# Products of p and v with the roles of the operands exchanged, in a kernel of attention and two expert layers

## Chip, cores, metric

The kernel runs on one core of a Trainium2 chip (trn2). The metric is the device time of one execution in microseconds; the median of several executions counts.

## What is computed

Attention keeps the 32 largest scores of each row, and its output goes through two layers. `B, heads, S, D` are 2, 8, 576, 64, so there are 1152 tokens of 512 features.

```python
scores = (q @ k.T) / sqrt(D)
kth = the 32nd largest score of each row
attn = softmax(where(scores >= kth, scores, -1e9))      # sum + 1e-9
x = attn @ v                       # (B, heads, S, D) -> (B * S, 512)

g = domain_probs / (sum(domain_probs) + 1e-9)
x = sum over e of g[:, e] * (relu(x @ w1[e]) @ w2[e])   # 4 experts, 1024 wide
out = max(x @ m1, x @ m2, x @ m3) @ mo                   # 768 wide
```

## The kernel before

**Pairs.** The tokens lie in nine tiles of 128, and tile 4 belongs half to each batch (it is the "mixed" tile). One unit of attention is a pair of heads for one tile: 36 pairs, class `Pair`, numbered 0 to 35 in the order of `pairs` (lines 371 and 372). The mixed tile's four pairs are numbers 16, 18, 20 and 21.

**Steps of a pair.** `scores` (TensorE, copied out by ScalarE); `topk`, seven VectorE steps for each head (max of 8 and replacement in turn, lines 444 and 446); `negate`, `exp` and `mask` make p and the sums of its rows; `trans_p` (lines 484 to 498) turns p in nine blocks of 128 x 128, and ScalarE copies them into `pt[0]`, `pt[1]` (four blocks each) and `pt[2]` (the last 64 keys of both heads together). `guard`, `recip` give the reciprocals `rr` of the sums, one for each token and head, tokens on partitions.

**Products with values, `pv`, lines 522 to 537.** The result stands transposed: partitions are the 2 x 64 features of the two heads, columns are tokens. v is the operand that stands in the array, p moves. The tail comes first, one matmul with 128 x 128 weights (`v_last`, block-diagonal), then for each of four blocks and two heads a matmul with 128 x 64 weights, whose results go to the partitions of that head:

```python
nc.tensor.matmul(ps[:, cols], lhsT=last, rhs=self.pt[2][:, cols], start=True, stop=False)
for r in range(NR):
    for j in range(2):
        nc.tensor.matmul(ps[j * D:(j + 1) * D, cols], lhsT=vs[:, j * NR + r, :],
                         rhs=self.pt[j][:, r, cols], start=False, stop=r == NR - 1)
```

A mixed pair does this twice, with 64 tokens of each batch. Since the result has features on partitions, the reciprocals have to be turned too: `spread` (line 513, ScalarE) repeats them to 128 x 128, `trans_r` (line 518, TensorE) transposes that, ScalarE copies it to `r` (line 520), and `norm` (line 542, VectorE) multiplies. `split_x` (lines 555 and 556) splits the result into a high part (ScalarE) and a low part (GpSimd), which lie in a ring of four tiles for the experts.

**Order.** Everything is issued in an order that the program fixes itself; each engine works through its queue in this order. `attention` counts in slots, eight for each pair, and puts every step at a slot from the pair's first: for most pairs (`LOOSE`, line 45) `recip` at 15, `pv` and `trans_r` at 17, the copy of r at 19, `norm` at 20, `split_x` at 21, with its GpSimd part at 23. `two` puts the second half of a step `lag` slots later. `last` says at which slot x of a pair counts as ready. The pairs 3, 7 and 11, the last of their tiles, and a few around them have tighter orders.

**Experts beside attention.** The first expert layer is a generator (`products`), from which the main loop (lines 992 to 1013) takes work slot by slot: the VectorE time that a slot books (`dve`) is added to a goal, and expert work is issued until the TensorE time it books (`pe`) reaches that goal. Where a stage needs x that isn't ready, nothing is issued and the goal's time is dropped. Stage c (1 to 6) works on tiles c − 1 and c, stages 7 and 8 on the last ones. Each product is three matmuls on split operands (`product`, lines 681 to 683). The second layer, with weights that VectorE, ScalarE and GpSimd convert after attention (`to_float32`), comes at the end. PSUM has six banks in one ring (tag "g") for all of these, and two for output sums.

Of the kernel before, what the change touches and what calls it, by code (L numbers as in the profile page):

```python
# [10 lines left out]
F32 = mybir.dt.float32  # L11
# [3 lines left out]
AF = mybir.ActivationFunctionType  # L15
ALU = mybir.AluOpType
# [11 lines left out]
WAITING = 2  # L28
# [6 lines left out]
ON_ACT = (range(2, 36), (2, 5, 6, 8, 9, 10, 12, 13, 14))  # L35
# [3 lines left out]
FIRST = dict(stag=2, new=1, scores=-12, trans=11, pv=17, rec=16, lag=2, sum=4, late=1)  # L39
MIDDLE = dict(stag=2, new=1, scores=-12, at=(11, 12), pv=14, rec=12, lag=1, sum=0, late=1)  # L40
TIGHT = dict(stag=3, new=1, scores=-7, at=(10, 11), guard=11, rec=11, spread=12, pv=12, turn=12, norm=13, split=13, last=14, lag=0, lag_s=1, sum=0, late=1)
SECOND = dict(TIGHT, norm=14, split=14, last=15)
THIRD = dict(stag=4, new=1, scores=-4, at=(11, 12), guard=12, rec=13, spread=13, pv=14, turn=14, norm=15, split=15, last=16, lag=0, lag_s=2, sum=0)
BOTH = dict(stag=4, new=1, scores=-4, at=(14, 14), pv=17, rec=15, lag=2, lag_t=1, sum=0, late=1)
LOOSE = dict(stag=4, new=1, scores=-4, at=(14, 14), pv=17, rec=15, lag=2, sum=0)

EARLY = 7

ALONE_FROM, ALONE_STEP = -8, 4
LOAD, LOAD_FULL = 11, 9  # L50
# [10 lines left out]
def kernel(  # L61
# [14 lines left out]
    nc = tc.nc  # L76
    B, HP, D, _, S = k.shape
    NT, DM = out.shape
    E = gates.shape[2]
    P = 128  # L80
# [3 lines left out]
    NR = S // P  # L84
# [27 lines left out]
    at = ctx.enter_context(tc.tile_pool(name="at", bufs=2))  # L112
# [7 lines left out]
    ident = const.tile([P, P], F32, name="ident")  # L120
# [9 lines left out]
    def dve(n):  # L130
        clock["dve"] += 0.07 + n / 960.0

    def pe(n):
        clock["pe"] += n / 2400.0

    def bank(name):
        return pg.tile([P, 512], F32, tag="g", name=name)
# [170 lines left out]
    kraw, kT, vt, qraw, qT = {}, {}, {}, {}, {}  # L308
# [85 lines left out]
    def split_waiting():  # L394
        while waiting and room(waiting[0].t):
            waiting.pop(0).split_x()()

    class Pair:
        def __init__(self, n):
            self.n = n  # L400
            self.c, self.hp, self.t = pairs[n]
            self.s, self.w, self.m, self.nb = {}, {}, {}, {}
            self.p = self.rs = None
            self.pt = {}

            self.did = set()

            self.on_pool = [n in ON_POOL[j] for j in range(2)]
            self.on_act = [n in ON_ACT[j] for j in range(2)]

        def scores(self, j):
            srcs = [(b, i) for i, b in enumerate(batches(self.t))]
# [109 lines left out]
        def pv(self):  # L522
            assert {("pt", i) for i in range(3)} <= self.did
            ps = bank("psv")
            pe((NR + 1) * 512)
            if self.t == MIXED:
                parts = [(0, slice(0, TAIL)), (1, slice(TAIL, P))]
            else:
                parts = [(0 if self.t < MIXED else 1, slice(0, P))]
            for b, cols in parts:  # L530
                vs, last = vt[b, self.hp]
                nc.tensor.matmul(ps[:, cols], lhsT=last, rhs=self.pt[2][:, cols], start=True, stop=False)
                for r in range(NR):
                    for j in range(2):
                        nc.tensor.matmul(ps[j * D:(j + 1) * D, cols], lhsT=vs[:, j * NR + r, :],
                                         rhs=self.pt[j][:, r, cols], start=False, stop=r == NR - 1)
            self.x = ps

        def norm(self):
            assert "r" in self.did  # L540
# [17 lines left out]
    def attention():  # L558

        NP = len(pairs)  # L560
        prs = {}
        later, between = {}, {}

        def options(n):
            return TIGHT if n == HP - 1 else SECOND if n == 2 * HP - 1 else MIDDLE if n in (HP - 2, 2 * HP - 3, 2 * HP - 2) else FIRST if n < 2 * HP else THIRD if n == 3 * HP - 1 else BOTH if n in ON_ACT[1] else LOOSE

        def at_slot(s, f, *a):
            later.setdefault(s, []).append((f, a))


        first_use = {}
        for n, (c, hp, t) in enumerate(pairs):
            for b in batches(t):
                if ("v", b, hp) not in first_use:
                    first_use["v", b, hp] = n
                    at_slot(8 * n + (options(n)["pv"] - 7 if b and hp else 0), load_v, b, hp)
                if t >= FULL:
                    first_use.setdefault(("k", b, hp), n)
            if t >= FULL:
                first_use.setdefault(("q", c, hp), n)  # L580
            elif n:
                o = options(max(0, n - 2))
                at_slot(max(8 * n + options(n)["scores"] - LOAD_FULL, 8 * (n - 2) + o["scores"] + o["stag"] + 1), load_full, n)
        free = {"k": -99, "q": -99}
        for key, n in first_use.items():
            if key[0] == "v":
                continue
            s0 = 8 * n
            load, split = (load_k, split_k) if key[0] == "k" else (load_q, split_q)
            at = max(s0 + options(n)["scores"] - (SPLIT_K if key[0] == "k" else SPLIT_Q), free[key[0]] + 2)  # L590
            if key[0] == "k" and key[1] and key[2]:

                at = max(at, 8 * pairs.index((MIXED, key[2] - 1, MIXED)) + options(n)["scores"] + options(n)["stag"] + (1 if key[2] == HP - 1 else 4))
            at_slot(max(at - LOAD, free[key[0]] + 1), load, *key[1:])
            at_slot(at, split, *key[1:])
            free[key[0]] = at
        for n, (c, hp, t) in enumerate(pairs):
            s0 = 8 * n
            prs[n] = Pair(n)
            pr = prs[n]  # L600
            o = options(n)

            def two(s, f, *a, lag=o["lag"]):
                at_slot(s, lambda: at_slot(s + lag, f(*a)))
            for j in range(2):
                b0 = s0 + o["stag"] * j
                two(b0 + o["scores"], pr.scores, j, lag=o.get("lag_s", o["lag"]))
                for i in range(7):
                    if o["new"]:
                        later.setdefault(b0 + i, []).insert(0, (pr.topk, (j, i)))  # L610
                    else:
                        at_slot(b0 + i, pr.topk, j, i)
                at_slot(b0 + 2, pr.negate, j)
                at_slot(b0 + 5, pr.exp, j)
                late = o.get("late", MASK_LATE) * pr.on_act[j]
                two(b0 + 7 + late, pr.mask, j, lag=o["sum"] if n < EARLY else 3)
                two(s0 + o["at"][j] if "at" in o else b0 + o["trans"] + late + (late > 0), pr.trans_p, j, lag=o.get("lag_t", o["lag"]))
            two(s0 + o["at"][1] if "at" in o else s0 + o["stag"] + o["trans"], pr.trans_p, 2, lag=o.get("lag_t", o["lag"]))
            at_slot(s0 + o.get("guard", o["rec"] - 1), pr.guard)
            at_slot(s0 + o["rec"], pr.recip)  # L620
            at_slot(s0 + o.get("spread", o["rec"] + 1), pr.spread)
            at_slot(s0 + o["pv"], pr.pv)
            two(s0 + o.get("turn", o["rec"] + 2), pr.trans_r)
            end = max(o["pv"], o["rec"] + 2) + o["lag"]
            if "norm" in o:
                between.setdefault(s0 + o["norm"], []).append((pr.norm, ()))
            else:
                at_slot(s0 + end + 1, pr.norm)
            two(s0 + o.get("split", end + 2), pr.split_x)
        last = {}  # L630
        for n, p in enumerate(pairs):
            o = options(n)
            last[p[0:2]] = 8 * n + o.get("last", max(o["pv"], o["rec"] + 2) + 2 * o["lag"] + 2)
        for n in range(len(alone)):
            at_slot(ALONE_FROM + ALONE_STEP * n, load_alone, n + 1)
        end = max(last.values()) + 1
        s = min(later)
        while s <= end:
            todo = later.pop(s, [])
            i = 0  # L640
            while i < len(todo):
                f, a = todo[i]
                f(*a)
                todo[i + 1:i + 1] = between.pop(s, [])
                todo += later.pop(s, [])
                i += 1
            yield s, [c for c in last if last[c] + (READY if c[1] == HP - 2 else 0) == s]
            s += 1

        while narrowed[0] < WIDE * len(wide):  # L650
            clock["dve"] += PAUSE
            yield s, []
            s += 1


    lag = []
# [424 lines left out]
```

## Time and profile before

| | |
|---|---|
| runs of the kernel, us | 751.1, 751.87, 753.61 |
| median, us | 751.87 |
| the profiled execution, us | 752.02 |
| its span, first to last instruction, us | 750.2 |
| granted clock of TensorE, mean | 0.997 |

The profile is of one execution. The span is shorter than that execution's own time by what lies around the instructions. A record is one instruction; busy time counts overlapping records of an engine once. PE is TensorE's matmul, PEld its weight load, DVE is VectorE, ACT ScalarE, POOL GpSimd. Starts of TensorE's records are the better guide: their ends are modelled. A number after L is the line of the kernel.

### The profile page before, as it was taken

How to read it: one execution, taken by the hardware profiler on the slowest of the kernel's cores; microseconds unless marked ns; L12 is line 12 of the kernel's file. 1: busy time of each engine (PE TensorE's matmuls, PEld its weight loads, DVE VectorE, ACT ScalarE, POOL GpSimd, SP SyncE). 2: the span in 40 equal slices, each digit the busy share in tenths (PEclk: the TensorE clock that was granted, in tenths of full speed). 3: DMA queues.
4: the chain of work that ended last, by engine and by line, in shares of the span. 5: the costliest groups of instructions: out<-in, count | busy, mean ns of one | idle time of the engine just before them, and what ended most of it. 6: DMA issues, size and time to landing. Idle time of an engine off the chain costs nothing. (4 is left out here: it accounts for less than half of the span.)

```text
span 750.2 us, 13770 instructions
## 1 busy us (share of the span) xinstructions
PE 721.8 (96%) x4758; PEld 642.7 (86%) x4758; DVE 579.1 (77%) x1161; ACT 508.0 (68%) x1137; POOL 495.2 (66%) x432
## 2 busy tenths in 40 slices
PE   6799999999999999999999998999999899999998
PEld 3576788888989989898989977899989799999996
DVE  6999989989999899999999964887778544233341
ACT  4668889899978787788788856576656633433531
POOL 2514778679979797697778659888768743442520
PEclk9999999999999999999999999999999999999999
DMA  7584565535647364445444355889979742453501
GB/s 221 179 267 158 154 183 159 154 127 159 192 123 212 110 189 124 149 134 166 134 132 153 114 183 168 298 297 301 297 239 314 257 149 82 151 172 99 195 4 42
DMA packets 56487, 130.16 MB, mean 173 GB/s; under 512 B 9761, under 2 KB 23329, under 8 KB 56417
## 3 DMA queue, kind: packets, MB, share of 16 engines
q1 hardware_dynamic: 48064, 120.69, 51.5%
q10 hardware_dynamic: 8352, 8.59, 3.2%
q8 instruction: 37, 0.61, 0.3%
q14 instruction: 34, 0.27, 0.1%
HBM read 120.60 MB, written 8.65 MB: 172 GB/s over the span
## 5 line engine op out<-in xcount | busy, mean ns | idle before, releaser
L278 POOL TENSOR_TENSOR wlo<-raw,whi 128x512 fp32r<-128x512 f32 x258 | 340.4, 1348 | 119.4 <-ACT whi L272 115.9
L272 ACT ACTIVATE whi<-raw 128x1024 fp32r<-128x1024 f32 x164 | 169.7, 1056 | 36.2 <-PE ps L683 12.9
L681 PE MATMUL ps<-xl,whi 128*128 128x256 f32 (+1 forms) x584 | 173.7, 297 | 0.4 <-POOL xl L556 0.4
L683 PE MATMUL ps<-xh,wlo 128*128 128x256 f32 (+1 forms) x584 | 170.8, 292 | 0.0
L682 PE MATMUL ps<-xh,whi 128*128 128x256 f32 (+1 forms) x584 | 170.7, 292 | 0.0
L444 DVE MAX8 m<-work 128x8 f32<-128x576 f32 x216 | 155.2, 745 | 0.1
L681 PEld LDWEIGHTS ps<-xl,whi 128*128 128x128 f32 x584 | 110.8, 190 | 1.7 <-POOL xl L556 0.6
L682 PEld LDWEIGHTS ps<-xh,whi 128*128 128x128 f32 x584 | 109.7, 188 | 0.8 <-issue 0.2
L683 PEld LDWEIGHTS ps<-xh,wlo 128*128 128x128 f32 x584 | 109.8, 188 | 0.0
L278 DVE TENSOR_TENSOR wlo<-raw,whi 128x1024 fp32r<-128x1024 f32 x35 | 56.2, 1606 | 66.3 <-ACT whi L272 48.9
L446 DVE MATCH_REPLACE8 work<-m,work 128x576 f32<-128x576 f32 x144 | 106.7, 742 | 0.0
L681 PE MATMUL ps<-wlo,h 128*128 128x512 f32 x224 | 91.1, 406 | 0.9 <-POOL wlo L278 0.9
L683 PE MATMUL ps<-whi,h 128*128 128x512 f32 x224 | 87.9, 393 | 3.5 <-POOL h L818 3.5
L682 PE MATMUL ps<-whi,h 128*128 128x512 f32 x224 | 87.8, 392 | 0.0
L431 ACT ACTIVATE s<-pss 128x288 f32<-128x288 f32 x144 | 51.2, 399 | 11.6 <-PE pss L419 11.1
L444 DVE MAX8 m<-s 128x8 f32<-128x576 f32 x72 | 53.8, 748 | 5.0 <-ACT s L431 5.0
L249 POOL TENSOR_TENSOR narrow<-narrow,raw 128x256 int32<-128x256 int32 x48 | 44.2, 927 | 17.1 <-DVE narrow L246 4.4
L683 PEld LDWEIGHTS ps<-whi,h 128*128 128x128 f32 x224 | 42.1, 188 | 13.9 <-POOL h L818 4.4
L446 DVE MATCH_REPLACE8 work<-m,s 128x576 f32<-128x576 f32 x72 | 53.4, 742 | 0.0
L681 PE MATMUL ps<-x2l,whi 128*128 128x384 f32 x144 | 49.1, 341 | 2.1 <-DVE x2l L908 2.1
L681 PEld LDWEIGHTS ps<-wlo,h 128*128 128x128 f32 x224 | 42.9, 192 | 9.1 <-POOL wlo L278 2.7
L683 PE MATMUL ps<-x2h,wlo 128*128 128x384 f32 x144 | 49.0, 341 | 0.0
(113 smaller groups left out, 1472.3 us busy)
## 6 DMA issues: line engine op xcount, KB each, us to landing
raw<-in_w_dram SPq DMA_DIRECT2D x128, 512.0 KB, 4.2
raw<-narrow SPq DMA_DIRECT2D x36, 512.0 KB, 4.0
raw<-in_m_dram SPq DMA_DIRECT2D x36, 256.0 KB, 4.7
whole<-in_w_dram SPq DMA_DIRECT2D x14, 512.0 KB, 5.4
narrow<-narrow ACTq DMA_DIRECT2D x48, 128.0 KB, 4.8
kraw<-in_k_dram SPq DMA_DIRECT2D x16, 288.0 KB, 4.5
qraw<-in_q_dram SPq DMA_DIRECT2D x48, 64.0 KB, 3.9
raw<-in_mo_dram SPq DMA_DIRECT2D x12, 256.0 KB, 4.7
```

The costliest lines, as they stand in the source:

```text
L249: nc.gpsimd.tensor_tensor(out=out.bitcast(I32), in0=out.bitcast(I32), in1=last, op=ALU.add)
L272: nc.scalar.activation(out=hi, in_=raw, func=AF.Copy)
L278: on.tensor_tensor(out=lo[:, x], in0=raw[:, x], in1=hi[:, x].bitcast(F32), op=ALU.subtract)
L431: nc.scalar.activation(out=s[:, h, :], in_=halves[h][:, 0:SH], func=AF.Copy)
L444: nc.vector.max(m[:, 8 * r:8 * r + 8], src)
L446: nc.vector.match_replace(out=self.w[j], in_to_replace=m[:, 8 * r:8 * r + 8], in_values=src, imm_value=NEG)
L681: nc.tensor.matmul(ps, lhsT=lh, rhs=rl, start=first, stop=False)
L682: nc.tensor.matmul(ps, lhsT=lh, rhs=rh, start=False, stop=False)
L683: nc.tensor.matmul(ps, lhsT=ll, rhs=rh, start=False, stop=last)
```

## The change

For the 26 pairs from number 8 on, but for 10 and 11, p's turned blocks stand in the array and v moves, 64 columns for a head. The result has tokens on partitions, so that `rr` scales it directly (`norm_tokens`); it is then transposed (`trans_x`) and copied by ScalarE. Such pairs have no `spread` and no `trans_r`. Their steps come at `pv` + 2 (multiplication), + 4 (transposition, copied `lag` slots later) and + 7 (split); x counts as ready at `pv` + 9. `options` is moved out of `attention` unchanged.

```diff
+TOKENS_FROM = 8
+TOKENS = dict(norm=2, turn=4, split=7, last=9)
...
+            self.tokens = n >= TOKENS_FROM and n not in (3 * HP - 2, 3 * HP - 1)
...
+            self.x = ps
+            if self.tokens:
+                for b, cols in parts:
+                    nc.tensor.matmul(ps[cols, 0:P], lhsT=self.pt[2][:, cols], rhs=vt[b, self.hp][1], start=True, stop=False)
+                for r in range(NR):
+                    for j in range(2):
+                        for b, cols in parts:
+                            nc.tensor.matmul(ps[cols, j * D:(j + 1) * D], lhsT=self.pt[j][:, r, cols],
+                                             rhs=vt[b, self.hp][0][:, j * NR + r, :], start=False, stop=r == NR - 1 and j == 1)
+                return
...
-            self.x = ps
+
+        def norm_tokens(self):
+            self.xn = at.tile([P, 2, D], F32, tag="rb", bufs=1, name="xn")
+            dve(P)
+            nc.vector.tensor_tensor(out=self.xn, in0=self.x[:, 0:P].rearrange("p (j d) -> p j d", j=2), in1=self.rr.unsqueeze(2).to_broadcast([P, 2, D]), op=ALU.mult)
+
+        def trans_x(self):
+            ps = bank("psr")
+            pe(260)
+            nc.tensor.transpose(ps[:, 0:P], self.xn.rearrange("p j d -> p (j d)"), ident)
+
+            def copy():
+                self.xt = at.tile([P, P], F32, tag="xt", bufs=2 + WAITING, name="xt")
+                nc.scalar.activation(out=self.xt, in_=ps[:, 0:P], func=AF.Copy)
+                self.did.add("x")
+            return copy
...
+            at_slot(s0 + o["pv"], pr.pv)
+            if pr.tokens:
+                at_slot(s0 + o["pv"] + TOKENS["norm"], pr.norm_tokens)
+                two(s0 + o["pv"] + TOKENS["turn"], pr.trans_x)
+                two(s0 + o["pv"] + TOKENS["split"], pr.split_x)
+                continue
             at_slot(s0 + o.get("spread", o["rec"] + 1), pr.spread)
-            at_slot(s0 + o["pv"], pr.pv)
             two(s0 + o.get("turn", o["rec"] + 2), pr.trans_r)
...
-            last[p[0:2]] = 8 * n + o.get("last", max(o["pv"], o["rec"] + 2) + 2 * o["lag"] + 2)
+            last[p[0:2]] = 8 * n + (o["pv"] + TOKENS["last"] if prs[n].tokens else o.get("last", max(o["pv"], o["rec"] + 2) + 2 * o["lag"] + 2))
```

## Rows read from the trace of the kernel before

**Rows 1.** The page, part 1: busy us, share of the span, instructions of each engine.

```profile
PE 721.8 (96%) x4758; PEld 642.7 (86%) x4758; DVE 579.1 (77%) x1161; ACT 508.0 (68%) x1137; POOL 495.2 (66%) x432
```

**Rows 2.** Busy time by stretch: length, PE, PEld, DVE, ACT, POOL, clock, DMA.

```profile
100.00:450.00 350.00, 342.41 (x2620) 307.89 (x2619) 326.46 (x695) 289.54 (x693) 277.97 (x246) 1.00 0.52 155
450.00:750.20 300.20, 292.08 (x1615) 270.48 (x1613) 161.18 (x265) 149.77 (x258) 174.98 (x140) 0.99 0.58 191
```

**Rows 3.** Waits, 100 to 447 us: who <- for whom: us, times, longest.

```profile
ACT rb L513 <- DVE rr L509: 25.8, 15, 3.1
ACT xh L555 <- DVE xt L542: 22.7, 17, 2.3
...
PE psv L532 <- ACT pt L498: 3.1, 4, 1.5
...
PE psp L495 <- ACT raw L816: 1.5, 2, 0.8
```

**Rows 4.** Timeline, TensorE, an ordinary pair's products: start, length, record, count.

```profile
251.42 0.38 PE L532 MATMUL psv<-pt,v_last 128*128 128x128 f32 x2
...
251.73 1.09 PE L535 MATMUL psv<-pt,vt 128*64 128x128 f32 x16
...
252.75 0.33 PE L518 MATMUL psr<-ident,rb 128*128 128x128 f32 x1
...
252.84 0.36 PE L681 MATMUL ps<-xl,whi 128*128 128x256 f32 x1
...
253.04 0.28 PE L682 MATMUL ps<-xh,whi 128*128 128x256 f32 x1
```

**Rows 5.** Timeline, TensorE, a mixed pair's products.

```profile
240.73 0.33 PE L532 MATMUL psv<-pt,v_last 128*128 128x64 f32 x2
240.99 0.69 PE L535 MATMUL psv<-pt,vt 128*64 128x64 f32 x16
241.61 0.43 PE L532 MATMUL psv<-pt,v_last 128*128 128x64 f32 x2
...
242.67 0.48 PE L681 MATMUL ps<-wlo,h 128*128 128x512 f32 x1
```

**Rows 6.** Weight loads: two in that pair (timeline), and their group.

```profile
241.61 0.30 PEld L532 LDWEIGHTS psv<-pt,v_last 128*128 128x128 f32 x2
...
L532 PEld LDWEIGHTS psv<-pt,v_last 128*128 128x128 f32 x80 | 12.8, 192 | 9.6 <-ACT pt L498 7.8 <-issue 0.5 <-ACT s L431 0.2
```

**Rows 7.** Timeline, TensorE, transpositions of p and the matmuls after them.

```profile
247.97 1.03 PE L490 MATMUL psp<-ident,p 128*128 128x128 f32 x8
248.84 0.27 PE L495 MATMUL psp<-ident,p 128*128 128x128 f32 x1
248.87 0.49 PE L681 MATMUL ps<-wlo,h 128*128 128x512 f32 x1
249.19 0.39 PE L682 MATMUL ps<-whi,h 128*128 128x512 f32 x1
```

**Rows 8.** TensorE's groups by form: busy us, mean ns of one; idle before.

```profile
L766 PE MATMUL psa<-xfull,whole 128*128 128x128 f32 x128 | 16.1, 279 | 0.8 <-ACT pt L493 0.8
...
L535 PE MATMUL psv<-pt,vt 128*64 128x64 f32 x128 | 5.5, 228 | 0.0
...
L532 PE MATMUL psv<-pt,v_last 128*128 128x64 f32 x16 | 3.2, 279 | 0.2 <-ACT pt L498 0.2
```

**Rows 9.** Groups by form: the spread on ScalarE, the multiplication on VectorE.

```profile
L513 ACT ACTIVATE rb<-rr 128x128 f32<-128x128 f32 x36 | 11.3, 313 | 29.5 <-DVE rr L509 29.2
...
L542 DVE TENSOR_TENSOR xt<-psv,r 128x128 f32<-128x128 f32 x32 | 8.7, 273 | 4.3 <-ACT r L520 4.3
```

**Rows 10.** TensorE's groups from 100 to 450 us: one transposition for each pair.

```profile
L518 PE MATMUL psr<-ident,rb 128*128 128x128 f32 x28 | 9.2, 328 | 0.0
```

**Rows 11.** Timeline: the low part of tile 4's last x; stage 4's first matmul.

```profile
283.65 0.46 POOL L556 TENSOR_TENSOR xl<-xt,xh 128x128 fp32r<-128x128 f32 x1 [2.56 <-ACT xh L555]
...
285.30 0.36 PE L681 MATMUL ps<-xl,whi 128*128 128x256 f32 x1
```

More of the change, by code (lines that the diff above doesn't have):

```diff
@@ L396, in split_waiting, with options @@
             waiting.pop(0).split_x()()
+    def options(n):
+        return TIGHT if n == HP - 1 else SECOND if n == 2 * HP - 1 else MIDDLE if n in (HP - 2, 2 * HP - 3, 2 * HP - 2) else FIRST if n < 2 * HP else THIRD if n == 3 * HP - 1 else BOTH if n in ON_ACT[1] else LOOSE
     class Pair:
@@ L562, in attention @@
         later, between = {}, {}
-        def options(n):
-            return TIGHT if n == HP - 1 else SECOND if n == 2 * HP - 1 else MIDDLE if n in (HP - 2, 2 * HP - 3, 2 * HP - 2) else FIRST if n < 2 * HP else THIRD if n == 3 * HP - 1 else BOTH if n in ON_ACT[1] else LOOSE
         def at_slot(s, f, *a):
```

## Prediction

> **What bounds the kernel now.** The page's busy shares come first: TensorE is busy for 721.8 of the span's 750.2 us, the next engine for 579.1 [rows 1]. A high share alone proves little, so the second view is busy time by stretch. From 100 to 450 us, where the attention of 28 pairs runs beside expert products, TensorE is busy for 342.4 of 350 us; from 450 us, when attention is over, for 292.1 of 300.2 [rows 2]. So there are only 7.6 us of idle time on TensorE in the stretch that the change touches, and work that is added to TensorE has nowhere to hide: the expert products that it pushes back come out at the end of the program. The third view, the waits of the same stretch, says how much of that idle time ScalarE causes: TensorE waits 3.1 us for copies of the transposed p and 1.5 us for a bank that ScalarE empties late. ScalarE itself stands 25.8 us before the spread of the reciprocals and 22.7 us before the split of x, both times for VectorE [rows 3].
>
> One execution carries all durations: its own time is 752.0 us, 1.8 us over its span, and 0.15 us over the median of the three runs, 751.87; I forecast against 752.0.
>
> **The products with values, ordinary pair** (22 of the 26 pairs). Each float32 matmul shows as two records, each with a weight load of its own. Now: the pair at 251.42 us issues one matmul with the tail of v (2 records, 128 columns of the array) and eight with v (16 records, 64 columns of the array each, the two heads side by side), then the transposition of the spread reciprocals; the next expert matmul starts at 252.84 and is 0.08 us longer than its neighbour (0.36 against 0.28), since it waits inside [rows 4]. The whole is 252.84 − 251.42 + 0.08 = **1.50 us**. The 16 records take 252.75 − 251.73 = 1.02 us, some 0.06 each, because two stream side by side.
>
> After: p stands still, so all 18 records load 128 x 128 float32 weights, and 64 columns stream past. Halving the columns helps only if loading is not the limit. The trace of before has this very shape: in a mixed pair the tail matmul loads 128 x 128 float32 weights for 64 columns. From its start to the first value matmul 240.99 − 240.73 = 0.26 us pass [rows 5]; with 128 columns it is 251.73 − 251.42 = 0.31 [rows 4]. Two records with 64 columns fewer each, at the 0.11 that a 128-column record takes (248.84 − 247.97 over 8) [rows 7], should have saved 0.11; they saved 0.05, one record's worth. The second record waited for its load. The loads say the same: two of 0.19 us take 0.30 together, so one ends 0.11 after the other [rows 6], and nothing streamed long enough there to hold the second back. And these 64-column records last 279 ns on average, where 64-column records with half the weights last 228 [rows 8].
>
> So I take 0.11 us a record: 18 x 0.11 = 1.98 us. Then the transposition of x, now by itself. The nearest row is the last one of p: 248.87 − 248.84 = 0.03, and the matmul behind it is 0.09 longer (0.49 against 0.40), so 0.12 [rows 7]. Together **2.10 us, 0.60 more than now; 22 pairs: +13.2 us**. Bounds for a record: 0.055, if streaming alone counted (half of 0.11; it gives a rival below), and 0.126, the mean of the 128-column records of L766, 16.1 us over 128 [rows 8], which adds 22 x 18 x 0.016 = 6.3 us. I stay at 0.11, the row with the same weights.
>
> The Trainium skill (TensorE: Matmul & The Clock Gate, Back-to-back issue gap) gives the isolated spacing of matmuls by the streamed columns alone, so that half the columns are half the time; its section LDWEIGHTS gives a load by its columns over 1.2 GHz, 107 ns for 128. By the first the sum would come to about 741 us, by the second (18 x 0.107 + 0.12 a pair) to about 761.5, both estimates from the page. The rows of loads agree with the second.
>
> **Mixed pairs** (4). Now 242.67 − 240.73 + 0.08 = 2.02 us [rows 5, 7]. After, the two batches take the two halves of the array, with the same 64-column weights as now, and the two entries into this arrangement become one. Entry 0.09 (the 0.31 of the tail matmul before v's records, less two of 0.11) [rows 4]; four tail records two by two, 0.22; 32 records with one leaving, 2 x 0.62 − 0.14 = 1.10 (0.62 from 240.99 to 241.61; leaving is 1.02 less 8 x 0.11 in the ordinary pair) [rows 4, 5]; transposition 0.12. Together 1.53: **4 x −0.49 = −2.0 us.** If the new order of the 32 records loses the side-by-side streaming they take 32 x 0.055 = 1.76 instead of 0.96, and the four pairs cost +1.2 in all; I take −2.0, since neighbours still go to different halves.
>
> **What leaves and enters elsewhere.** The spread (0.31 us of ScalarE) goes in 26 pairs, and with it the wait for the reciprocal ahead of it; the copy of r becomes a copy of x, the same shape; the split then reads what ScalarE itself wrote, so its wait for VectorE goes too [rows 3, 9]. That is 26 x 0.31 = 8.1 us of work and most of 48.5 us of standing still, on an engine that isn't the bound. It counts only where TensorE waits for ScalarE: 3.1 + 1.5 us [rows 3]. Bounds 0 and −4.6; I take **−2.0**. The multiplication on VectorE keeps its shape (0.27 us, one factor now repeated along the row) [rows 9], moves one slot earlier and waits for the products instead of the copy of r; what queues behind it are the top-k steps of the next pairs, which TensorE must not come to need. It now also books 0.203 us in the planner's VectorE clock, 5.3 us in 26 pairs, which pulls as much expert work forward into attention; that moves work and adds none. No DMA is added or moved within a pair.
>
> **x later.** Transposition and split move x of a token pair from slot 23 to slot 26 after its pair's start. There are 28 pairs in 350 us [rows 10], so 12.5 us for a pair's 8 slots, and three slots are 4.7 us. Who waits is the next expert stage. Where x has time, this costs nothing; stage 4, however, begins at 285.30, 1.2 us after the last low part of tile 4 is written (283.65 + 0.46) [rows 11]. In the 3.5 us beyond this margin TensorE has only the attention's own work, roughly a third of its time by the pattern of scores, transpositions and products; so 0 to 2.3 us of idling. I take **+1.0**, because a TensorE that runs later than the plan spends part of it catching up. After the last pair, nothing stands between products and transposition, so TensorE waits for the multiplication of 0.27 us and its hand-over: **+0.5**, between 0 and 1.
>
> Sum: 752.0 + 13.2 − 2.0 − 2.0 + 1.0 + 0.5 = 762.7, so **763 us**.
>
> **Rivals.**
> - *Loads hide, streaming counts* (the other side). For it: the starts of the two 64-column records can't be told apart from a streaming cadence in a row that merges them, and loads do overlap matmuls everywhere. Against it: the 0.26, 0.30 and 279 above. A pair would take 18 x 0.055 + 0.12 = 1.11 us; 22 x −0.39 = −8.6, and with the other terms 752.0 − 8.6 − 2.0 − 2.0 + 1.5 = 741 us. The sign turns at 0.083 us a record: there 22 x (18 x 0.083 + 0.12 − 1.50) = 2.5 us, what the other terms (−2.5) give back. This is what the skill's rule on the issue gap would give (TensorE: Matmul & The Clock Gate). Chance 0.09.
> - *The idle time takes it.* TensorE fills all of its 7.6 idle us [rows 2] with the added work and the late x costs nothing: 752.0 + 13.2 − 2.0 − 7.6 = 755.6, and with records of 0.105, 753.6, no change that can be told. For it: ScalarE's freed 48 us. Against it: only 4.6 of the waits are ScalarE's. Chance 0.05, 0.04 of it within 0.3%.
> - *The late x decides.* Stage 4 pays its full 2.3, the multiplication on VectorE waits for slower products and holds up the top-k behind it once in most pairs, and records cost 0.115: 762.7 + 1.3 + 22 x 18 x 0.005 + 1 = 767 us. For it: the 1.2 us at stage 4 [rows 11]. Against it: the multiplication still comes two slots, 3.1 us, after the products, which grow by half a microsecond. Chance 0.12.
> - The forecast itself: 0.74. That the change does something else than it says is not a case: the loads, their shapes and the 26 pairs are plain from the code.
>
> **The numbers.** The likeliest case gives 763. The range runs from 755, where idle time takes most of it, to 769, where the late x or the higher price of a record decides; the faster rival is left out. About 0.3% (2.3 us) is what a measurement of this kernel can tell from no change. Faster 0.09, same 0.04, slower 0.87.
>
> **What would show it.** Right: the records of the new products stand 0.11 us apart and their loads touch each other without gaps; a token pair takes about 2.0 us on TensorE before it turns to other work; TensorE's busy time rises by about 11 us, while idle time in attention shrinks a little; spread and its 25.8 us of waiting are gone but for a few pairs; attention ends 15 us or so later, the rest is shorter. Wrong: records 0.06 apart (the first rival), a stop of TensorE by 285 to 300 us for x of 2 us or more (the third), a mixed pair above 2.0 us (side-by-side streaming lost).

## The result and the profile after

The changed kernel takes 763.37 us (median; 761.29 to 765.17), the kernel before 752.74 us beside it: a ratio of 1.0139, 95% interval 1.0106 to 1.0172. It is slower by 10.6 us, and the forecast of 763 us holds. The profiled execution took 765.17 us, with a span of 763.4 us, so its rows show some 2 us more than the median.

First come the products of an ordinary pair, in the timeline of TensorE and its weight loads (start, length, record, count). L541 is the tail's matmul and L545 the eight with v.

```profile
256.79 0.32 PEld L541 LDWEIGHTS psv<-v_last,pt 128*128 128x128 f32 x2
256.92 0.39 PE L541 MATMUL psv<-v_last,pt 128*128 128x128 f32 x2
257.03 1.87 PEld L545 LDWEIGHTS psv<-vt,pt 128*128 128x128 f32 x16
...
257.14 1.90 PE L545 MATMUL psv<-vt,pt 128*128 128x64 f32 x16
...
258.82 0.19 PEld L717 LDWEIGHTS ps<-xl,whi 128*128 128x128 f32 x1
258.85 0.36 PE L717 MATMUL ps<-xl,whi 128*128 128x256 f32 x1
```

From 256.92 to 258.85 us, 18 records take 1.93 us, 0.107 each. The row of loads has 16 loads of 0.19 us in 1.87 us with no break: (1.87 − 0.19) / 15 = 0.112 from one to the next. Loads are now back to back, and streaming seems to wait for them (the first experiment tests it). Before, the same work took 1.33 us up to the transposition [rows 4]. A mixed pair, whose weights have 64 columns, is quicker than before: 273.63 − 272.33 = 1.30 us, with the transposition still to come, against 1.94 us that hold the transposition [rows 5]:

```profile
272.33 0.44 PE L541 MATMUL psv<-v_last,pt 128*64 128x128 f32 x4
272.60 1.10 PE L545 MATMUL psv<-vt,pt 128*64 128x64 f32 x32
273.63 0.39 PE L717 MATMUL ps<-xl,whi 128*128 128x256 f32 x1
```

Then the page and busy time by stretch (columns as in [rows 1, 2]).

```profile
PE 737.6 (97%) x4758; PEld 665.2 (87%) x4758; DVE 580.4 (76%) x1161; ACT 509.2 (67%) x1111; POOL 494.3 (65%) x432
```

```profile
100.00:450.00 350.00, 344.58 (x2540) 318.65 (x2539) 323.33 (x683) 283.59 (x653) 277.84 (x244) 1.00 0.50 150
...
100.00:465.00 365.00, 357.70 (x2634) 330.43 (x2633) 329.96 (x700) 291.75 (x674) 280.42 (x248) 1.00 0.50 148
465.00:763.40 298.40, 291.73 (x1615) 270.19 (x1613) 160.59 (x264) 150.09 (x257) 172.78 (x140) 0.99 0.59 193
```

TensorE's busy time rose by 15.8 us, where the forecast had about 11, and VectorE's hardly at all. (The version with 128 columns below, whose profile has a mean clock of 0.997 like the one of before, is busy for 733.9 us, 12.1 more; the profile here, at 0.995, holds more slow records.) In the same 350 us TensorE idles for 5.4 us instead of 7.6, but attention now lasts until some 465 us, and up to there it idles for 7.3: idle time took up next to nothing. Behind attention the same 1615 matmul records stand in 298.4 us, and in 300.2 before [rows 2]: attention has grown by some 15 us, and the end moved with it.

ScalarE's two long waits, 25.8 and 22.7 us [rows 3], are gone but for 1.0 and 1.6 us in the groups from 100 to 450 us. New is a wait of 10.2 us for the transposition of x:

```profile
L588 ACT ACTIVATE xh<-xt 128x128 fp32r<-128x128 f32 x27 | 8.5, 314 | 2.1 <-DVE xt L575 1.6
L568 ACT ACTIVATE xt<-psr 128x128 f32<-128x128 f32 x24 | 6.7, 279 | 10.2 <-PE psr L564 10.2
L521 ACT ACTIVATE rb<-rr 128x128 f32<-128x128 f32 x2 | 0.6, 314 | 1.0 <-DVE rr L517 1.0
```

TensorE's own waits from 100 to 465 us show what that is worth to it. Those for copies of p are down to 1.8 us from 3.1, and that for a bank that ScalarE empties to 0.4 from 1.5 [rows 3]:

```profile
PE ps L717 <- POOL xl L589: 2.4, 2, 1.7
PE psv L541 <- ACT pt L506: 1.6, 2, 1.1
...
PE psp L503 <- ACT raw L852: 0.4, 1, 0.4
PE psv L550 <- ACT pt L506: 0.2, 1, 0.2
```

Stage 4, which began 1.2 us after its x [rows 11], now waits for it. The timeline of TensorE, with idle time and its releaser in brackets:

```profile
292.95 0.28 PE L718 MATMUL ps<-xh,whi 128*128 128x256 f32 x1
293.06 0.28 PE L719 MATMUL ps<-xh,wlo 128*128 128x256 f32 x1
295.05 0.56 PE L717 MATMUL ps<-xl,whi 128*128 128x256 f32 x1 [1.72 <-POOL xl L589]
295.42 0.42 PE L718 MATMUL ps<-xh,whi 128*128 128x256 f32 x1
295.63 0.41 PE L719 MATMUL ps<-xh,wlo 128*128 128x256 f32 x1
```

After the wait the same matmuls stand 0.21 us apart instead of 0.11. The row of the stretch shows why: the granted clock (third from the end) is 0.58 on average from 296 to 299 us, so TensorE ran mostly at the lower of its two levels, 1.2 GHz.

```profile
296.00:299.00 3.00, 3.00 (x18) 3.00 (x17) 2.78 (x6) 2.78 (x5) 3.00 (x3) 0.58 0.02 5
299.00:302.00 3.00, 3.00 (x27) 3.00 (x27) 2.73 (x6) 2.06 (x6) 3.00 (x3) 1.00 0.58 175
```

### The profile page after: what moved, and what is told of

Read it like the earlier page. It is cut to its first block, busy times and chain, and to the rows that moved or that the text cites. A ratio compares the mean times of both kernels' runs of the same rounds, so it can differ in the third digit from the quotient of the medians.

```text
span 763.4 us, 13738 instructions
## 1 busy us (share of the span) xinstructions
PE 737.6 (97%) x4758; PEld 665.2 (87%) x4758; DVE 580.4 (76%) x1161; ACT 509.2 (67%) x1111; POOL 494.3 (65%) x432
## 4 chain that ended last, share of the span: by engine, by line
PE 89%; ACT 4%; issue 3%; POOL 3%; DVE 1%; DMA 0%; ACTq 0%; POOLq 0%
PE ps L717 21%; PE ps L719 20%; PE ps L718 20%; PE psv L545 5%; PE pss L432 4%; PE psp L498 4%; PE pss L427 3%; PE psa L802 2%; PE pso L717 2%; PE pso L718 2%; PE pso L719 2%; PE psv L553 1%; PE ps L817 1%; POOL wlo L281 1%; PE psv L541 1%
## 5 line engine op out<-in xcount | busy, mean ns | idle before, releaser
L501 ACT ACTIVATE pt<-psp 128x512 f32<-128x512 f32 x72 | 39.8, 595 | 16.9 <-PE psp L498 16.8
```

Of the source, the lines that this page charges most:

```text
L501: return lambda: [nc.scalar.activation(out=d, in_=ps.rearrange("p (r n) -> p r n", r=NR), func=AF.Copy), self.did.add(("pt", part))]
```

## The experiments

**Is it the load or the streaming?** Two kernels change only how many columns pass each block of p in the 22 ordinary pairs: 32 (the other half of each head's v is left out) or 128 (the v of both heads) instead of 64.

```diff
-                            nc.tensor.matmul(ps[cols, j * D:(j + 1) * D], lhsT=self.pt[j][:, r, cols],
-                                             rhs=vt[b, self.hp][0][:, j * NR + r, :], ...)
+                            n = D // 2 if len(parts) == 1 else D
+                            nc.tensor.matmul(ps[cols, j * D:j * D + n], lhsT=self.pt[j][:, r, cols],
+                                             rhs=vt[b, self.hp][0][:, j * NR + r, 0:n], ...)
```

> The changed kernel, but in the 22 ordinary pairs only 32 of the 64 columns of each head stream past the standing blocks of p (the other 32 get the tail's part alone, so part of the products is left out). Theory (a record waits for its 128 x 128 weight load, 0.107 us whatever streams): the 18 records still take 1.92 us, the time stays at 763 us within 2. Rival (the 0.107 us are the streaming of 64 columns): 16 records of 0.053 us, 0.85 us less a pair, 22 pairs: 745 us.

```diff
+                            if len(parts) == 1:
+                                nc.tensor.matmul(ps[cols, 0:P].rearrange("p (j d) -> p j d", j=2), lhsT=self.pt[j][:, r, cols],
+                                                 rhs=vt[b, self.hp][0][:, r::NR, :], ...)
+                                continue
```

> The changed kernel, but in the 22 ordinary pairs 128 columns (both heads of v) stream past each block of p instead of 64, so each head's result also gets the products of the other head's p. Theory (load-bound): streaming 128 columns takes 0.109 us a record, as long as the load, so the 18 records take 1.92 to 1.96 us and the time stays at 763 to 764 us. Rival (streaming sets 0.107 us for 64 columns): 0.213 us a record, 16 x 0.107 x 22 = 38 us more, 801 us.

With 32 columns the median is 765.13 us (ratio 1.0168, 1.0141 to 1.0195), with 128 columns 761.76 us (1.0128, 1.0111 to 1.0145). The small difference goes against the number of columns, and three of the four runs with 32 columns had a low mean granted clock (0.989 to 0.991): at 0.995 the two took 762.51 and 761.98 us. The timelines of both, 32 columns first:

```profile
319.87 1.87 PE L546 MATMUL psv<-vt,pt 128*128 128x32 f32 x16
321.57 0.47 PE L718 MATMUL ps<-wlo,h 128*128 128x512 f32 x1
```

```profile
317.72 1.95 PE L546 MATMUL psv<-vt,pt 128*128 128x128 f32 x16
319.42 0.48 PE L721 MATMUL ps<-wlo,h 128*128 128x512 f32 x1
```

Sixteen records take 1.70 us with 32 columns, 1.70 with 128, and 1.71 with 64 in the changed kernel. So 32 to 128 columns cost the same, and the forecast's reading of the two tail records [rows 5] was right: streaming doesn't set the pace; by it the two kernels would have lain 56 us apart. A fixed cost of every record, whatever it loads, would look the same here; the next experiment excludes it.

**Two half loads side by side.** The ordinary pair is made as the mixed pair already was, with p's block as two halves of 64 tokens side by side.

```diff
             if self.tokens:
+                if len(parts) == 1:
+                    parts = [(parts[0][0], slice(0, D)), (parts[0][0], slice(D, P))]
                 for b, cols in parts:
```

> The changed kernel, but an ordinary pair's products are made like a mixed pair's: p's blocks stand as two halves of 64 tokens side by side, 36 records instead of 18, with the same 64 columns of v each. Theory (the loss is the weight load of 128 columns; two loads of 64 columns go side by side): an ordinary pair falls from 1.92 us to the 1.30 us of a mixed pair, 22 x 0.62 = 13.7 us less, 749 to 751 us, at or below the kernel before. Rival (the loss is the later x and the changed order): nothing falls, 763 us.

752.54 us; ratio 0.9997, 0.9984 to 1.0010. Of the loss 10.8 us are gone. The timeline of an ordinary pair shows 36 records in 327.57 − 326.27 = 1.30 us, where 18 took 1.93:

```profile
326.27 0.44 PE L543 MATMUL psv<-v_last,pt 128*64 128x128 f32 x4
326.54 1.10 PE L547 MATMUL psv<-vt,pt 128*64 128x64 f32 x32
327.57 0.50 PE L719 MATMUL ps<-wlo,h 128*128 128x512 f32 x1
```

That takes both halving and going side by side: 18 pairs of records at 0.107 us each would take 1.93 us again, and so would 36 half loads one behind the other at half of it (estimates from these rows). A record's time falls with the columns that are loaded, so it isn't a fixed cost of every record; what sets the pace of the whole blocks is the load.

The sum had promised 13.7 us. Of the rest some 1 us is idle time, and what the other 2 us are isn't shown. Attention ends by 450 us here, and TensorE is busy for 341.6 of the 350 us from 100 us on; it idles for 8.4 us where the changed kernel idles for 7.3 up to 465 us, and its waits for x grew from 2.4 to 3.1 us:

```profile
100.00:450.00 350.00, 341.58 (x3006) 308.64 (x3005) 326.89 (x694) 287.60 (x667) 280.99 (x245) 1.00 0.52 155
```

```profile
PE ps L719 <- POOL xl L591: 3.1, 2, 2.4
```

**The later x.** Products as in the changed kernel, but the steps behind them moved up, so that x is ready at the slot of before.

```diff
-TOKENS = dict(norm=2, turn=4, split=7, last=9)
+TOKENS = dict(norm=2, turn=3, split=5, last=6)
...
-                two(s0 + o["pv"] + TOKENS["turn"], pr.trans_x)
-                two(s0 + o["pv"] + TOKENS["split"], pr.split_x)
+                two(s0 + o["pv"] + TOKENS["turn"], pr.trans_x, lag=1)
+                two(s0 + o["pv"] + TOKENS["split"], pr.split_x, lag=1)
```

> The changed kernel with the same products, but the transposition one slot earlier, copied one slot after, the split at pv + 5 with its second part one slot later, and x ready at pv + 6, as before the change. Theory: the products still cost some 11 to 13 us; what goes is TensorE's wait of 1.7 us for x at 293 us and the 3.4 us at half clock behind it (about 1.5 us): 760 us. Rival (the later x is most of the loss): 753 to 755 us. Third possibility (no slack for the transposition three slots after the products): more waits, 764 us or above.

758.32 us; ratio 1.0081, 1.0065 to 1.0096. The earlier x is worth 5.0 us, more than the 3.2 expected, and this version still loses 6 us to the kernel before. Stage 4's wait is gone. (One wait for x is left in attention, 0.8 us at 151 us; the changed kernel has it too, 0.7 us at 153 us.) Another wait that goes lies shortly behind attention. In the changed kernel TensorE waits there for a low part from GpSimd, and the clock falls behind this wait too (0.58 on average from 472 to 476 us):

```profile
471.73 0.50 PE L719 MATMUL ps<-whi,h 128*128 128x512 f32 x1 [1.74 <-POOL h L854]
```

```profile
472.00:476.00 4.00, 4.00 (x12) 3.08 (x12) 2.53 (x5) 1.25 (x3) 4.00 (x5) 0.58 0.63 177
```

With the early x that wait is not among those of TensorE. But the later x didn't bring it: the kernel before waits at the same place, for 2.24 us, and keeps its clock.

```profile
456.93 0.50 PE L683 MATMUL ps<-whi,h 128*128 128x512 f32 x1 [2.24 <-POOL h L818]
```

```profile
454.00:460.00 6.00, 3.76 (x17) 2.77 (x16) 3.04 (x7) 2.22 (x5) 6.00 (x6) 1.00 0.65 227
```

So a part of the 5.0 us is a wait of the kernel before, and not a cost of the change. Another part goes with the clock: the four runs with early x had a mean of 0.997 or 0.998. The version with 128 columns, whose products take as long and whose x is late, took 761.53 and 762.76 us at 0.997, which is 3.2 to 4.5 us more.

**ScalarE's relief.** To the version with early x the spread of the reciprocals is given back in all 26 pairs, its result unused. It is written to the buffers of `r`, which such pairs don't need.

```diff
-            self.rb = at.tile([P, 2, D], F32, tag="rb", bufs=1, name="rb")
+            self.rb = at.tile([P, 2, D], F32, tag="r" if self.tokens else "rb", bufs=2 if self.tokens else 1, name="rb")
...
             if pr.tokens:
+                at_slot(s0 + o.get("spread", o["rec"] + 1), pr.spread)
                 at_slot(s0 + o["pv"] + TOKENS["norm"], pr.norm_tokens)
```

> The version with x as early as before and whole blocks of p, plus the spread of the reciprocals on ScalarE put back in the 26 pairs, its result unused: 8.1 us of ScalarE's work and its wait for VectorE return, nothing else. By my term for ScalarE 2 us more than without, 760 us, between 758 (ScalarE is not the bound, the relief is worth nothing) and 763 us (it is worth all 4.6 us of TensorE's waits).

762.94 us; ratio 1.0149, 1.0110 to 1.0187. So 4.6 us more than without, at the upper end of what was expected. The waits from 100 to 465 us show the spread's own wait back on ScalarE, and TensorE's for the copies of p doubled, to 2.1 us from 1.0:

```profile
ACT rb L521 <- DVE rr L517: 26.9, 18, 3.4
...
PE psv L541 <- ACT pt L506: 2.1, 3, 1.5
```

TensorE's waits of this stretch add up to 7.4 us against 5.3, which explains 2.1 of the 4.6 us. Where the rest comes from stays open. The run with a mean granted clock of 0.999 took 760.53 us, 2.2 more than without the spread, but the one at 0.998, the clock of the runs without it, took 762.55 us, 4.2 more.

**Both repairs, and what each pair is worth.** Three versions were run together: halves and early x in all 26 pairs; the same without pairs 34 and 35; and early x with only the four mixed pairs changed.

```diff
-            self.tokens = n >= TOKENS_FROM and n not in (3 * HP - 2, 3 * HP - 1)
+            self.tokens = n >= TOKENS_FROM and n not in (3 * HP - 2, 3 * HP - 1) and n < len(pairs) - 2
```

```diff
-            self.tokens = n >= TOKENS_FROM and n not in (3 * HP - 2, 3 * HP - 1)
+            self.tokens = self.t == MIXED
```

> Both repairs together: p's blocks as two halves of 64 tokens, and x as early as before the change. If the two losses add, the 752.5 us of the halves fall by what the earlier x gave alone, 4 to 5 us: 748 us, 0.5% under the kernel before. If VectorE, 327 of 350 us busy in attention, now paces it, the gain is lost there: 751 to 753 us.

> The same, but the last two pairs, 34 and 35, as before the change. In them TensorE waits 0.46 us each between products and transposition, since nothing else is queued there, while products and transpositions of both kinds cost the same 1.50 us: 0.9 us less than with them, some 747 us. If those waits were idle time anyway: no difference.

> Only the four mixed pairs changed, x as early as before. Their products and transposition take 1.50 us instead of 2.02: 4 x 0.52 = 2.1 us less, 750 us. What the version with halves in all pairs gains beyond this comes from elsewhere, since an ordinary pair costs TensorE 1.50 us either way: by my forecast from ScalarE's missing spread and waits, 2 us. If ScalarE's relief counts for nothing, both versions take the same time.

They took 748.84 us (ratio 0.9957, 0.9937 to 0.9978), 746.58 us (0.9935, 0.9910 to 0.9960) and 751.78 us (0.9996, 0.9973 to 1.0020). The two losses nearly add: halves and early x together are 3.7 us below halves alone. Leaving out the last two pairs gained 2.3 us by the medians, but at a granted clock of 0.999 or 1.000 the two versions take 747.13 to 747.32 and 746.34 to 746.58 us (and once 748.36): about the 0.9 us expected, and the rest goes with the clock. The mixed pairs alone missed their 2.1 us. At 1.000 two of three runs took 749.2 and 749.3 us, some 0.5 less than the kernel before beside them (most of its runs 749.6 to 749.8). TensorE has less to do, but idles more, 8.6 of the 350 us against 7.6 [rows 2], while VectorE is busy for 327.4 of them:

```profile
100.00:450.00 350.00, 341.45 (x2619) 306.19 (x2619) 327.42 (x695) 289.11 (x689) 278.68 (x246) 1.00 0.51 155
```

The step from this version to halves in all pairs, 2.9 us, doesn't come from TensorE's products, since an ordinary pair costs it nearly the same either way (1.30 and a transposition after, 1.50 with it before). It fits ScalarE's relief; that this is the cause is argued, not shown.

**The best version again, and what it books.** It was run again, and beside it without the 0.203 us that the multiplication books in the planner's VectorE clock.

```diff
             self.xn = at.tile([P, 2, D], F32, tag="rb", bufs=1, name="xn")
-            dve(P)
```

> The version with halves, early x and the last two pairs as before the change, measured once more with more runs: 746 to 748 us, 0.5 to 0.8% under the kernel before. If its first measurement was a lucky one, 749 us or more.

> The same without the 0.203 us that the multiplication books in the planner's VectorE clock for each pair of the new kind (24 pairs, 4.9 us less expert work pulled into attention). If booking only moves work, as I had it: the same within 1 us. If attention is short of TensorE work without it (VectorE is 325 of 350 us busy there): up to 3 us more, 750 us. If it crowds attention: less than 746 us.

746.56 us (ratio 0.9947, 0.9921 to 0.9973), so this version does beat the kernel before, by half a per cent. Without the booking it takes 750.51 us (0.9971, 0.9958 to 0.9985): 4.0 us more, where the forecast had said that booking moves work and adds none. The timeline without it shows TensorE waiting behind attention for GpSimd's low part, as in the kernel before, a wait that the version with booking doesn't have:

```profile
454.76 0.50 PE L720 MATMUL ps<-whi,h 128*128 128x512 f32 x1 [2.29 <-POOL h L855]
```

At a granted clock of 1.000 the two take 746.5 and 748.6 us, a difference about as long as this wait. So booking is worth 2.1 us at an equal clock, and the rest of the 4.0 goes with the clock: without booking 8 of 12 runs were at 0.995 or 0.997 and took 750.3 to 750.9. The kernel before takes 749.7 at 1.000. Of the 3.2 us by which the best version is below it there, about two thirds go together with that wait, which is a matter of the order, and 1.1 us are left for everything else.

## Why the prediction was right, and where it was lucky

- **The record's price**, on which all rested, is shown. 0.11 was forecast, 0.107 measured, and with 32 and 128 columns it stays the same. The first rival, streaming, is refuted. The Trainium skill (TensorE: Matmul & The Clock Gate, LDWEIGHTS) gives the time of a load by its columns over 1.2 GHz, an estimated 107 ns for 128 columns. The records' spacing agrees, 0.106 to 0.107 us, while a single load's record lasts 0.19 us.
- **The ordinary pair**: 2.10 us forecast. Measured: 1.93, 0.08 that the next matmul waits (0.36 against 0.28), and a transposition, for which 0.12 was taken; 2.13. (The 0.12 goes with 0.40 for a neighbour whose row says 0.39 [rows 7], a matter of 0.01 us.) The two loads in a mixed pair's tail were the right row to read.
- **The mixed pair**: forecast 1.53 with transposition; measured 1.30, 0.11 of waiting (0.39 against 0.28) and the same 0.12. Right on TensorE. But the forecast booked all of it as time won, and in the run with mixed pairs alone it was not: about 1 us of the 2.1 came back as idle time of TensorE. That VectorE, nearly as full, is the reason is argued only.
- **x later** was mis-sized: +1.0 us, at most 2.3, in the sum. The mechanism and the place were right (stage 4, a wait of 1.72 us). Missing were the slow matmuls behind the wait: 15 records took 3.35 us there, from 295.05 to 298.40 us, and would take some 1.8 at 0.12 each. With the wait that is some 3.2 us. Making x early gave 5.0, but this took away a wait behind attention too, which the kernel before has as well.
- **ScalarE's relief**: −2.0 forecast, bounds 0 and −4.6. In the changed kernel TensorE's waits of the two kinds fell from 4.6 to 2.2 us, which agrees. Giving the spread back cost 4.6 us, of which 2.1 are waits of TensorE and the rest is open; the other half of the relief, the split's wait, isn't in that experiment.
- **Booking** was costed at nothing. In the best version it is worth 4.0 us, 2.1 at an equal clock. It wasn't tried in the changed kernel itself.
- **The last pair**: +0.5 forecast, and right. TensorE waits for the multiplication between products and transposition, 0.38 us in this timeline of the changed kernel, and pair 34 has a wait of the same length:

```profile
459.61 1.90 PE L545 MATMUL psv<-vt,pt 128*128 128x64 f32 x16
461.55 0.29 DVE L559 TENSOR_TENSOR xn<-psv,rr 128x128 f32<-128x128 f32 x1 [3.76 <-PE psv L545]
461.89 0.33 PE L564 MATMUL psr<-ident,xn 128*128 128x128 f32 x1 [0.38 <-DVE xn L559]
```

So the likeliest case happened, for the reason that was given: of 10.6 us lost, splitting the weights alone takes back 10.8. That the sum met the median within 0.4 us is partly luck. The four runs lie between 761.29 and 765.17 us, the late x cost some 2 us more than forecast and the ordinary pairs 0.7 us more (22 x 0.03). What gave this back isn't shown; a larger relief of ScalarE and the booking are candidates. Of the third rival, stage 4's stop came true, 1.72 us of its 2.3, but the rest didn't: records cost 0.107 and not 0.115, and although VectorE's multiplication waited 13.0 us for products in 11 of the pairs, TensorE waited for VectorE for only 0.8 us from 100 to 465 us.

## To carry to other kernels

Before exchanging the operands of a float32 matmul, price the weight load of the new shape beside the streaming, from a row that already has many columns of weights and few that stream: here 128 x 128 weights cost 0.107 us a record whether 32, 64 or 128 columns pass. If the result is wanted that way round, split the standing block into halves that load and stream side by side: that took back the whole loss here. The 0.5% that the best version is ahead came with steps behind the products kept on time, and at an equal clock about two thirds of it go with an order in which one wait of 2 us is gone. And when a bounding engine is relieved in a stretch where another is nearly as full, look for the gain as idle time before counting it.

## What the runs showed that was not expected

A wait of about 2 us on TensorE can cost twice. Behind the waits of 1.72 and 1.74 us the granted clock fell to the lower of its two levels for some 3.4 us, and records of 256 columns stood 0.1 us further apart there, those of 512 columns 0.2. It is not tied to waits of this length: with early x the clock was 0.59 on average from 458 to 461 us, where the longest wait just before was 0.96 us. Nor does it follow every such wait. The best version waits 2.05 us for the second layer's first x and keeps its clock, as the timeline and the stretch behind show:

```profile
588.42 0.41 PE L719 MATMUL ps<-x2l,whi 128*128 128x384 f32 x1 [2.05 <-DVE x2l L946]
```

```profile
588.00:592.00 4.00, 3.58 (x21) 3.61 (x22) 3.93 (x8) 0.72 (x2) 4.00 (x3) 1.00 0.92 304
```

Before the change the same place, with a wait of the same length, had a granted clock of 0.59:

```profile
592.00:596.00 4.00, 3.29 (x10) 3.32 (x11) 3.97 (x8) 1.48 (x3) 4.00 (x4) 0.59 0.97 349
```

This goes with much of the scatter between runs of one kernel. In the last set of the kernel before, those at 1.000 took 749.7 and 749.8 us, those at 0.995 between 751.7 and 754.2; the changed kernel took 761.29 at 1.000 and 762.72 to 765.17 at 0.995 and 0.996. It isn't all of it: one run of the kernel before took 756.07 us at 1.000, and two of the best version 754.55 and 754.79 at 0.995 and 0.997. Medians of these kernels thus compare how often the clock falls as well as how much work there is.
